# Sliding-window attention and a GEGLU block on one core: attention of the next batch interleaved by hand with an FFN group, sums by a ones matmul

## Chip, core and metric

One core of a Trainium2 chip runs the whole program. The metric is the device time of one execution in microseconds (us), as the median of several runs; every profile here is of one execution.

## What is computed

Eight batches of eight heads, 576 tokens of 64 features each, go through attention with a window of 128 tokens and a bias that grows with distance (ALiBi). The result, seen as 4608 tokens of 512 features, goes through a gated feed-forward block (FFN) of width 1536.

```python
scores = scale * np.matmul(q, k.transpose(0, 1, 3, 2))
mask = (rel >= 0) & (rel < window)                 # rel = query - key, window 128
scores = np.where(mask, scores + bias[None], -1e9)
attn = np.exp(scores - max); attn = attn / (np.sum(attn) + 1e-09)
x = np.matmul(attn, v)                             # as (4608, 512)
out = (gelu(x @ w_gate) * (x @ w_val)) @ w_out     # (4608, 512) float32
```

## The kernel before

**Attention** (attention_bp, L104 to L214) takes two batches at a time. POOL issues the loads of q, k and v (L113, L132), which change float32 to bf16 on the way. TensorE (PE) transposes q and k in blocks of 128 tokens (L98), and evac (L88 to L93) copies them out of PSUM on ACT (L90) and DVE (L92) in turn. For each head there are five key blocks: two score matmuls (L158, one for each batch), an exp on ACT over both (L164), a multiplication with the exponential of bias and mask on DVE (L168). Then come the value matmuls (L185). There the probabilities are the stationary operand and the values move, 65 columns: 64 values and a column of ones, so that the 65th output column is the sum over the keys, one number per query. DVE takes the reciprocal of these sums, four columns on 128 partitions and one on 64 (L192, L193), and multiplies the outputs by them (L195, L201). The result has tokens on partitions, so it is transposed once more (L98) into xT, which has features on partitions.

**The FFN** (ffn_group, L216 to L246) takes 512 tokens, nine groups in all. For each of 12 blocks of the hidden width four matmuls make the gate (L222), ACT takes gelu (L227), four make the value (L231), DVE multiplies the two (L235). Then four token blocks take 12 matmuls each with w_out (L240), evac copies them out, SP stores them (L246). PSUM has eight banks: three for scores, two for attention outputs, two for gate and value, one for the FFN's output (L45 to L48).

**Order.** The calls at the end (L248 to L258) go: attention of batches 0 and 1, the weight loads (L249 to L251), FFN groups 0 and 1, attention of 2 and 3, groups 2 and 3, and so on, with groups 6, 7 and 8 at the end. The scheduler of the framework may move instructions within an engine's queue: it pulls transposes of the next pair of batches into the FFN.

Of the kernel before, what the change touches and what calls it, by code (L numbers as in the profile page):

```python
# [10 lines left out]
ALU = mybir.AluOpType  # L12


@with_exitstack
def kernel(
# [10 lines left out]
    nc = tc.nc  # L27
# [5 lines left out]
    NKT = (S + 127) // 128  # L33
    LAST = S - 128 * (NKT - 1)

    consts = ctx.enter_context(tc.tile_pool(name="consts", bufs=1))
    slab_pool = ctx.enter_context(tc.tile_pool(name="slabs", bufs=2))
    qkT_pool = ctx.enter_context(tc.tile_pool(name="qkT", bufs=3))
    v_pool = ctx.enter_context(tc.tile_pool(name="vp", bufs=3))
    pT_pool = ctx.enter_context(tc.tile_pool(name="pT", bufs=3))  # L40
    xnat_pool = ctx.enter_context(tc.tile_pool(name="xnat", bufs=2))
    r_pool = ctx.enter_context(tc.tile_pool(name="rp", bufs=4))
    ffn_sb = ctx.enter_context(tc.tile_pool(name="ffn_sb", bufs=3))
    out_sb_pool = ctx.enter_context(tc.tile_pool(name="out_sb", bufs=3))
    ps_sc = ctx.enter_context(tc.tile_pool(name="ps_sc", bufs=3, space=bass.MemoryType.PSUM))  # L45
    ps_o = ctx.enter_context(tc.tile_pool(name="ps_o", bufs=2, space=bass.MemoryType.PSUM))
    ps_gv = ctx.enter_context(tc.tile_pool(name="ps_gv", bufs=2, space=bass.MemoryType.PSUM))
    ps_out = ctx.enter_context(tc.tile_pool(name="ps_out", bufs=1, space=bass.MemoryType.PSUM))  # L48

    ident = consts.tile([128, 128], BF16)  # L50
    nc.gpsimd.memset(ident, 0.0)
    nc.gpsimd.affine_select(
        out=ident, in_=ident, compare_op=ALU.not_equal, fill=1.0,
        base=0, pattern=[[-1, 128]], channel_multiplier=1,
    )

# [6 lines left out]
    nc.gpsimd.affine_select(
        out=tmpl, in_=tmpl, compare_op=ALU.is_ge, fill=1e9,
        base=0, pattern=[[1, 256]], channel_multiplier=-1,
    )
    nc.gpsimd.affine_select(
        out=tmpl, in_=tmpl, compare_op=ALU.is_ge, fill=1e9,
        base=W - 1, pattern=[[-1, 256]], channel_multiplier=1,
    )  # L70
# [3 lines left out]
    init_pool.release()  # L74

    wg = consts.tile([128, 4, DFF], BF16)
    wv = consts.tile([128, 4, DFF], BF16)
    wo = consts.tile([128, 12, DM], BF16)

    xT = consts.tile([128, 4, NTOK], BF16)  # L80

    qspan = [(128 * j, min(256, S - 128 * j)) for j in range(NKT)]
    pslot = [256 * j for j in range(NKT)]
    PTW = 256 * (NKT - 1) + LAST

    evac_flip = [0]

    def evac(dst, src):  # L88
        if evac_flip[0] % 2 == 0:
            nc.scalar.copy(out=dst, in_=src)  # L90
        else:
            nc.vector.tensor_copy(out=dst, in_=src)  # L92
        evac_flip[0] += 1  # L93

    def pe_transpose_block(ps_bf16, src):
        for j in range(NKT):
            sz = 128 if j < NKT - 1 else LAST
            nc.tensor.transpose(  # L98
                out=ps_bf16[:, 128 * j:128 * j + sz],
                in_=src(j, sz),  # L100
                identity=ident[0:sz, 0:sz],
            )

    def attention_bp(bp):  # L104
        bb = (2 * bp, 2 * bp + 1)
        qT, kT, vnat, xnat = {}, {}, {}, {}
        for b in bb:
            qsb = slab_pool.tile([128, NKT, DM], BF16, name="qsb")
            ksb = slab_pool.tile([128, NKT, DM], BF16, name="ksb")
            for sb, src in ((qsb, q), (ksb, k)):  # L110
                for j in range(NKT):
                    sz = 128 if j < NKT - 1 else LAST
                    nc.gpsimd.dma_start(  # L113
                        out=sb[0:sz, j, :].rearrange("p (h d) -> p h d", h=H),
                        in_=src[b][:, 128 * j:128 * j + sz, :].rearrange(
                            "h p d -> p h d"),
                    )

            qT[b] = qkT_pool.tile([128, 4, S], BF16, name="qT")
            kT[b] = qkT_pool.tile([128, 4, S], BF16, name="kT")  # L120
            for sb, dst in ((qsb, qT[b]), (ksb, kT[b])):
                for c in range(4):
                    pst = ps_sc.tile([128, 512], FP32, name="sc")
                    pstb = pst.bitcast(BF16)
                    pe_transpose_block(
                        pstb, lambda j, sz: sb[0:sz, j, 128 * c:128 * (c + 1)])
                    evac(dst[:, c, :], pstb[:, 0:S])

            vsb = slab_pool.tile([128, NKT, DM], BF16, name="vsb")
            for j in range(NKT):  # L130
                sz = 128 if j < NKT - 1 else LAST
                nc.gpsimd.dma_start(  # L132
                    out=vsb[0:sz, j, :].rearrange("p (h d) -> p h d", h=H),
                    in_=v[b][:, 128 * j:128 * j + sz, :].rearrange(
                        "h p d -> p h d"),
                )
            vnat[b] = v_pool.tile([128, NKT, H, 65], BF16, name="vp")
            nc.vector.memset(vnat[b][:, :, :, 64:65], 1.0)  # L138
            nc.vector.tensor_copy(
                out=vnat[b][:, 0:NKT - 1, :, 0:64],  # L140
                in_=vsb[:, 0:NKT - 1, :].rearrange("p j (h d) -> p j h d", h=H),
            )
            nc.vector.tensor_copy(
                out=vnat[b][0:LAST, NKT - 1, :, 0:64],
                in_=vsb[0:LAST, NKT - 1, :].rearrange("p (h d) -> p h d", h=H),
            )
            xnat[b] = xnat_pool.tile([128, NKT, DM], BF16, name="xnat")

        for h in range(H):
            hc, hp = h // 2, (h % 2) * 64  # L150
            pT = pT_pool.tile([128, 2, PTW], BF16)
            for j in range(NKT):
                kp = 128 if j < NKT - 1 else LAST
                q0, nq = qspan[j]
                sc = ps_sc.tile([128, 512], FP32, name="sc").rearrange(
                    "p (x n) -> p x n", x=2)
                for i, b in enumerate(bb):
                    nc.tensor.matmul(  # L158
                        out=sc[0:kp, i, 0:nq],
                        lhsT=kT[b][hp:hp + 64, hc, 128 * j:128 * j + kp],  # L160
                        rhs=qT[b][hp:hp + 64, hc, q0:q0 + nq],
                        start=True, stop=True,
                    )
                nc.scalar.activation(  # L164
                    out=pT[0:kp, :, pslot[j]:pslot[j] + nq],
                    in_=sc[0:kp, :, 0:nq], func=AF.Exp, scale=0.125,
                )
                nc.vector.tensor_tensor(  # L168
                    out=pT[0:kp, :, pslot[j]:pslot[j] + nq],
                    in0=pT[0:kp, :, pslot[j]:pslot[j] + nq],  # L170
                    in1=emask[0:kp, h:h + 1, 0:nq].to_broadcast((kp, 2, nq)),
                    op=ALU.mult,
                )

            for i, b in enumerate(bb):
                opp = ps_o.tile([128, NKT, 65], FP32, name="opp")
                for qt in range(NKT):
                    qs = 128 if qt < NKT - 1 else LAST
                    mms = []
                    if qt > 0:  # L180
                        mms.append((qt - 1, pslot[qt - 1] + 128))
                    mms.append((qt, pslot[qt]))
                    for mi, (j, col) in enumerate(mms):
                        kp = 128 if j < NKT - 1 else LAST
                        nc.tensor.matmul(  # L185
                            out=opp[0:qs, qt, :],
                            lhsT=pT[0:kp, i, col:col + qs],
                            rhs=vnat[b][0:kp, j, h, :],
                            start=(mi == 0), stop=(mi == len(mms) - 1),
                        )  # L190
# [98 lines left out]
```

## Time and profile before

| What | Value |
|---|---|
| Time, median of 3 runs | 528.34 us (527.97 to 529.66) |
| Span of the profiled execution, first to last instruction | 527.3 us |
| PE busy, share of the span | 487.2 us, 92% |
| DVE busy | 205.2 us, 39% |
| ACT busy | 188.4 us, 36% |
| POOL busy | 105.7 us, 20% |

The page gives no other time of the profiled execution than its span. Busy times of PE contain the time that a matmul takes to run through, and matmuls overlap, so 92% does not mean that PE streams at its peak. A group of instructions is named by engine and line of the kernel above; "idle before" is the time its engine stood still ahead of it, with what ended that.

### The profile page before, as it was taken

To read this page: it belongs to the slowest core of one execution; us is meant where nothing else is said; L and a number is where in the kernel's file an instruction comes from. 1 tells how busy PE (TensorE), PEld (TensorE's weight loads), DVE (VectorE), ACT (ScalarE), POOL (GpSimd) and SP (SyncE) were. 2 spreads that over 40 slices of the span, in tenths; PEclk is the share of its full clock that TensorE was granted. 3 is DMA by queue.
4 is the path that set the end of the run, shared out by engine and by line. 5 is a ranking of instruction groups with operands and counts; after the bars stand their busy time and mean duration, and the time that the engine had idled before them with its cause. 6 is when DMAs were issued, how large, how long until landed. Compare 5 with 4: busy or idle time off the path is not lost.

```text
span 527.3 us, 6826 instructions
## 1 busy us (share of the span) xinstructions
PE 487.2 (92%) x2638; PEld 239.9 (45%) x2672; DVE 205.2 (39%) x614; ACT 188.4 (36%) x350; POOL 105.7 (20%) x133
## 2 busy tenths in 40 slices
PE   3499899999989899999899999999899899999995
PEld 1255554444555544444555544444455434444432
DVE  0255644333354653142345643232354633232331
ACT  3166243132365243122565152132565232132220
POOL 9961796300440030002720000000000000000000
PEclk9999999999955589999955599999855589999999
DMA  9999999910990070102990000101100000201102
GB/s 88 138 178 210 158 142 101 106 40 2 125 90 1 0 47 0 61 20 31 167 63 2 0 1 1 73 8 41 42 0 1 0 1 0 81 1 41 40 0 81
DMA packets 120336, 28.76 MB, mean 55 GB/s; under 512 B 113136, under 2 KB 114672, under 8 KB 120304
## 3 DMA queue, kind: packets, MB, share of 16 engines
q0 software_dynamic: 115120, 18.88, 47.2%
q1 hardware_dynamic: 5184, 9.44, 4.7%
q8 instruction: 21, 0.34, 0.3%
q14 instruction: 11, 0.09, 0.0%
HBM read 37.75 MB, written 9.44 MB: 89 GB/s over the span
## 4 chain that ended last, share of the span: by engine, by line
PE 80%; DMA 6%; POOL 5%; ACT 4%; DVE 3%; issue 1%; another core or an unknown queue 1%; DVEq 0%; POOLq 0%; ACTq 0%
PE gv L231 20%; PE gv L222 17%; PE po L240 17%; PE opp L185 10%; PE sc L158 8%; PE sc L98 7%; DMA wv<-in_moe_w_val_dram 4%; DMA ksb<-in_k_dram 2%; POOL ksb L113 2%; POOL vsb L132 2%; POOL qsb L113 1%; ACT pT L164 1%; DVE hT L235 1%; ACT L164 1%
## 5 line engine op out<-in xcount | busy, mean ns | idle before, releaser
L235 DVE TENSOR_TENSOR hT<-gv,gelu 128x512 bf16<-128x512 f32 x108 | 74.7, 692 | 116.3 <-PE gv L231 111.9
L222 PE MATMUL gv<-xT,wg 128*128 128x512 bf16 x419 | 112.9, 388 | 2.4 <-ACT gelu L227 2.0
L231 PE MATMUL gv<-xT,wv 128*128 128x512 bf16 x420 | 112.6, 385 | 2.3 <-DVE hT L235 1.0
L227 ACT ACTIVATE gelu<-gv 128x512 bf16<-128x512 f32 x108 | 64.5, 597 | 133.5 <-PE gv L222 124.4
L240 PE MATMUL po<-wo,hT 128*128 128x512 bf16 x423 | 98.5, 379 | 2.7 <-ACT osb L90 1.3
L164 ACT ACTIVATE pT<-sc 128x512 bf16<-128x512 f32 (+2 forms) x160 | 71.2, 513 | 44.0 <-PE sc L158 27.5
L158 PE MATMUL sc<-qT,kT 64*128 64x256 bf16 (+2 forms) x320 | 75.0, 354 | 6.1 <-ACT pT L164 5.2
L185 PE MATMUL opp<-vp,pT 128*128 128x65 bf16 (+2 forms) x576 | 75.6, 246 | 4.3 <-DVE xnat L201 4.1
L231 PEld LDWEIGHTS <-wv 128*128 128x128 bf16 x432 | 42.4, 98 | 65.7 <-issue 27.5
L185 PEld LDWEIGHTS <-pT 128*128 128x128 bf16 (+2 forms) x576 | 46.9, 122 | 42.3 <-issue 11.8
L222 PEld LDWEIGHTS <-wg 128*128 128x128 bf16 x432 | 42.0, 98 | 52.3 <-issue 3.6
L240 PEld LDWEIGHTS <-hT 128*128 128x128 bf16 x432 | 41.8, 98 | 52.0 <-issue 4.0
L168 DVE TENSOR_TENSOR pT<-pT,emask 128x512 bf16<-128x512 bf16 (+2 forms) x160 | 48.5, 359 | 6.1 <-ACT pT L164 5.6
L113 POOL DMA_DIRECT2D qsb<-in_q_dram x40 | 34.4, 897 | 59.3 <-PE sc L98 59.1
L113 POOL DMA_DIRECT2D ksb<-in_k_dram x40 | 33.8, 888 | 54.4 <-PE sc L98 35.7
L92 DVE COPY osb<-po 128x512 f32<-128x512 f32 x18 | 12.5, 692 | 80.4 <-PE po L240 75.1
L132 POOL DMA_DIRECT2D vsb<-in_v_dram x40 | 34.0, 895 | 47.2 <-DVE vp L138 38.6
L158 PEld LDWEIGHTS <-kT 64*128 64x128 bf16 (+1 forms) x320 | 31.2, 122 | 26.0 <-issue 10.2
L192 DVE RECIPROCAL r<-opp 128x4 f32<-128x4 f32 x64 | 10.8, 176 | 61.5 <-PE opp L185 61.0
L90 ACT COPY osb<-po 128x512 f32<-128x512 f32 x18 | 10.5, 585 | 67.5 <-PE po L240 64.5
L98 PE MATMUL sc<-ident,qsb 128*128 128x128 bf16 (+1 forms) x160 | 19.2, 242 | 14.5 <-DMA qsb<-in_q_dram 13.2
L90 ACT COPY xT<-sc 128x576 bf16<-128x576 bf16 x16 | 10.2, 638 | 46.3 <-PE sc L98 46.3
(33 smaller groups left out, 198.4 us busy)
## 6 DMA issues: line engine op xcount, KB each, us to landing
out_dram<-osb SPq DMA_DIRECT2D x36, 256.0 KB, 2.0
qsb<-in_q_dram POOLq DMA_DIRECT2D x32, 128.0 KB, 4.4
ksb<-in_k_dram POOLq DMA_DIRECT2D x32, 128.0 KB, 4.9
vsb<-in_v_dram POOLq DMA_DIRECT2D x32, 128.0 KB, 4.1
wg<-in_moe_w_gate_dram POOLq DMA_DIRECT2D x1, 1536.0 KB, 12.1
wv<-in_moe_w_val_dram POOLq DMA_DIRECT2D x1, 1536.0 KB, 18.7
wo<-in_moe_w_out_dram POOLq DMA_DIRECT2D x1, 1536.0 KB, 25.6
qsb<-in_q_dram POOLq DMA_DIRECT2D x8, 64.0 KB, 4.0
```

The lines of the kernel that those rows point to most:

```text
L98: nc.tensor.transpose(out=ps_bf16[:, 128 * j:128 * j + sz], in_=src(j, sz), identity=ident[0:sz, 0:sz],)
L113: nc.gpsimd.dma_start(out=sb[0:sz, j, :].rearrange("p (h d) -> p h d", h=H), in_=src[b][:, 128 * j:128 * j + sz, :].rearrange("h p d -> p ...
L132: nc.gpsimd.dma_start(out=vsb[0:sz, j, :].rearrange("p (h d) -> p h d", h=H), in_=v[b][:, 128 * j:128 * j + sz, :].rearrange("h p d -> p h ...
L158: nc.tensor.matmul(out=sc[0:kp, i, 0:nq], lhsT=kT[b][hp:hp + 64, hc, 128 * j:128 * j + kp], rhs=qT[b][hp:hp + 64, hc, q0:q0 + nq], start=T ...
L164: nc.scalar.activation(out=pT[0:kp, :, pslot[j]:pslot[j] + nq], in_=sc[0:kp, :, 0:nq], func=AF.Exp, scale=0.125,)
L168: nc.vector.tensor_tensor(out=pT[0:kp, :, pslot[j]:pslot[j] + nq], in0=pT[0:kp, :, pslot[j]:pslot[j] + nq], in1=emask[0:kp, h:h + 1, 0:nq] ...
L185: nc.tensor.matmul(out=opp[0:qs, qt, :], lhsT=pT[0:kp, i, col:col + qs], rhs=vnat[b][0:kp, j, h, :], start=(mi == 0), stop=(mi == len(mms) ...
L222: nc.tensor.matmul(out=pg, lhsT=wg[:, c, 128 * f:128 * (f + 1)], rhs=xT[:, c, t0:t0 + 512], start=(c == 0), stop=(c == 3),)
L227: nc.scalar.activation(out=gelu, in_=pg, func=AF.Gelu)
L231: nc.tensor.matmul(out=pv, lhsT=wv[:, c, 128 * f:128 * (f + 1)], rhs=xT[:, c, t0:t0 + 512], start=(c == 0), stop=(c == 3),)
L235: nc.vector.tensor_tensor(out=hT[:, f, :], in0=pv, in1=gelu, op=ALU.mult)
L240: nc.tensor.matmul(out=po, lhsT=hT[:, f, 128 * t:128 * (t + 1)], rhs=wo[:, f, :], start=(f == 0), stop=(f == 11),)
```

## The change

The kernel is rewritten, with the order of the five engines' instructions fixed by hand (the order in the program is the order in each queue). Attention handles one batch and, within it, a pair of heads (c = 0 to 3) at a time. q and k are transposed as before. Keys are shifted by 64, so that the five key blocks meet 192, 256, 256, 256 and 128 queries (NQ). Score matmuls of the two heads alternate between the upper and lower 64 rows of the array and write two banks. Value matmuls have the values as the stationary operand, 64 columns for each head in its own half of the array's columns, and the probabilities move; the output comes out with features on partitions, as xT wants it, so the transposes after attention go. The sums over keys come from a second set of the same matmuls with a matrix of ones as stationary operand: every one of 64 partitions of a head then holds the sum of each query. Thus the reciprocal runs over 320 and 256 columns on 128 partitions. Eight PSUM banks are one pool. The mask of key blocks 0, 3 and 4 has its own table, emask2. Attention of batch g+1 runs within FFN group g: its transposes between the blocks of gate and value, the rest between halves of the output matmuls (6 each). Groups 7 and 8 have no attention beside them. The column ones and the weights' loads in four slices are set up at the start.

```diff
+NQ = (192, 256, 256, 256, 128)
+Q0 = (0, 64, 192, 320, 448)
+PCOL = (768, 0, 256, 512, 960)
+QS = 320
...
+    ctx.enter_context(tc.manual_schedule(
+        engines={ENG.PE, ENG.Activation, ENG.DVE, ENG.Pool, ENG.SP}))
...
+    psum = ctx.enter_context(
+        tc.tile_pool(name="psum", bufs=8, space=bass.MemoryType.PSUM))
+    def bank():
+        return psum.tile([128, 512], FP32, name="ps")
...
+    def score(b, c, i, j, ps, col):
+        lo = 64 * i
+        nc.tensor.matmul(
+            out=ps[:, col:col + NQ[j]],
+            lhsT=kT[b % 2][lo:lo + 64, c, 128 * j:128 * j + 128],
+            rhs=qT[b % 2][lo:lo + 64, c, Q0[j]:Q0[j] + NQ[j]],
+            start=True, stop=True)
...
+    def scores0(b, c):
+        ps = [bank(), bank()]
+        for m in (0, 1):
+            for i in (0, 1):
+                score(b, c + m, i, 4, ps[i], 128 * m)
+        for i in (0, 1):
+            exp(P[:, :, i, 960:1088], ps[i][:, 0:256].rearrange("p (m n) -> p m n", m=2))
+    def scores1(b, c):
+        ps = [bank(), bank()]
+        for j in (1, 2):
+            for i in (0, 1):
+                score(b, c, i, j, ps[i], PCOL[j])
+        for i in (0, 1):
+            exp(P[:, i, 0:512], ps[i])
+        mask(P[:, :, 0:512].rearrange("p i (n x) -> p i n x", n=2),
+             emask[:, 2 * c:2 * c + 2, :].unsqueeze(2).to_broadcast((128, 2, 2, 256)))
+    def scores2(b, c):
+        ps = [bank(), bank()]
+        for j in (0, 3):
+            for i in (0, 1):
+                score(b, c, i, j, ps[i], PCOL[j] - 512)
+        for i in (0, 1):
+            exp(P[:, i, 512:960], ps[i][:, 0:448])
+        mask(P[:, :, 512:1088], emask2[:, 2 * c:2 * c + 2, :])
+    def values(b, c):
+        x, y, z = bank(), bank(), bank()
+        for what in (0, 1):
+            for j in range(5):
+                for (a, e, ps, base) in (
+                        (Q0[j], min(Q0[j] + NQ[j], QS), (x, z)[what], 0),
+                        (max(Q0[j], QS), Q0[j] + NQ[j], y, 256 * what - QS)):
...
+                    for i in (0, 1):
+                        col = PCOL[j] + a - Q0[j]
+                        w = (vb[b % 2][:, j, 64 * (2 * c + i):64 * (2 * c + i) + 64]
+                             if what == 0 else ones)
+                        nc.tensor.matmul(
+                            out=ps[64 * i:64 * i + 64, base + a:base + e],
+                            lhsT=w, rhs=P[:, i, col:col + e - a],
+                            start=first, stop=last, skip_group_check=True)
+        r = r_pool.tile([128, S], FP32, name="r")
+        nc.vector.reciprocal(r[:, 0:QS], z[:, 0:QS])
+        nc.vector.tensor_tensor(out=xT[:, c, t0:t0 + QS], in0=x[:, 0:QS],
+                                in1=r[:, 0:QS], op=ALU.mult)
+        nc.vector.reciprocal(r[:, QS:S], y[:, 256:512])
+        nc.vector.tensor_tensor(out=xT[:, c, t0 + QS:t0 + S], in0=y[:, 0:256],
+                                in1=r[:, QS:S], op=ALU.mult)
...
+    load_qk(0)
...
+    load_v(0)
...
+    for h in range(H):
+        nc.scalar.activation(out=emask[:, h, :], in_=tmpl, func=AF.Exp, scale=-slope)
+    nc.vector.tensor_copy(out=emask2[:, :, 0:256], in_=emask)
+    nc.vector.memset(emask2[0:64, :, 256:448], 0.0)
+    nc.vector.tensor_copy(out=emask2[64:128, :, 256:448], in_=emask[64:128, :, 64:256])
+    nc.vector.tensor_copy(out=emask2[:, :, 448:576], in_=emask[:, :, 0:128])
+    for s in range(4):
+        load_w(step * s, step * (s + 1))
+    load_qk(1)
+    load_v(1)
+    nc.gpsimd.dma_start(out=wo, in_=moe_w_out.rearrange("(c p) f -> p c f", p=128))
+    for c in range(4):
+        if c % 2 == 0:
+            for m in (c, c + 1):
+                transposes(0, m)
+                transposes(0, 4 + m)
+            scores0(0, c)
+        scores1(0, c)
+        scores2(0, c)
+        if c:
+            values(0, c - 1)
+    values(0, 3)
+    for g in range(NG):
+        b = g + 1
+        if 1 < b < B:
+            load_qk(b)
+            load_v(b)
+        for f in range(NF):
+            gate_val(g, f)
+            if b < B and 2 <= f < 10:
+                transposes(b, f - 2)
+        if b < B:
+            scores0(b, 0)
+            scores1(b, 0)
+            out_half(g, 0)
+            scores2(b, 0)
+            out_half(g, 1)
+            scores1(b, 1)
+            out_half(g, 2)
+            scores2(b, 1)
+            values(b, 0)
+            out_half(g, 3)
+            scores0(b, 2)
+            scores1(b, 2)
+            out_half(g, 4)
+            scores2(b, 2)
+            values(b, 1)
+            scores1(b, 3)
+            out_half(g, 5)
+            scores2(b, 3)
+            values(b, 2)
+            out_half(g, 6)
+            values(b, 3)
+            out_half(g, 7)
+        else:
+            for u in range(8):
+                out_half(g, u)
```

transposes, gate_val and out_half do the same work as the old transposes, gate and value blocks and output blocks; out_half(g, u) is 6 of the 12 matmuls of token block u // 2, and the second half of each is copied out by DVE or ACT in turn and stored.

## Rows read from the trace of the kernel before

**Rows 1.** The page: span, busy time of PE and DVE, granted clock in 40 slices

```profile
span 527.3 us, 6826 instructions
...
PE 487.2 (92%) x2638; PEld 239.9 (45%) x2672; DVE 205.2 (39%) x614; ACT 188.4 (36%) x350; POOL 105.7 (20%) x133
...
PEclk9999999999955589999955599999855589999999
```

**Rows 2.** Stretches: start:end, length, busy of PE, PEld, DVE, ACT, POOL, clock, DMA

```profile
66.67:144.34 77.67, 76.60 (x385) 35.83 (x392) 27.97 (x54) 23.75 (x39) 31.46 (x38) 1.00 0.99 85
144.34:183.79 39.45, 36.22 (x243) 20.86 (x244) 21.77 (x99) 20.73 (x44) 6.69 (x9) 0.53 0.48 32
...
523.33:527.30 3.97, 0.00 (x0) 0.00 (x0) 0.69 (x1) 0.00 (x0) 0.00 (x0) 1.00 0.17 66
```

**Rows 3.** The chain that ended last: start, length, what; FFN matmuls

```profile
78.01 1.01 PE gv L231 x4
79.02 0.86 PE gv L222 x4
79.89 1.01 PE gv L231 x4
...
99.20 2.59 PE po L240 x12
```

**Rows 4.** Reciprocals that follow each other, near 60.24 us: groups of instructions

```profile
L192 DVE RECIPROCAL r<-opp 128x4 f32<-128x4 f32 x1 | 0.2, 154 | 0.0
L193 DVE RECIPROCAL r<-opp 64x1 f32<-64x1 f32 x1 | 0.1, 128 | 0.0
```

**Rows 5.** One line's instructions: all reciprocals of L192 and of L193, minimum/median/maximum

```profile
L192 DVE RECIPROCAL r<-opp x64: 154/182/184, 34.3 to 415.8; 128x4 f32<-128x4 f32 x64
...
L193 DVE RECIPROCAL r<-opp x64: 127/140/152, 34.4 to 416.3; 64x1 f32<-64x1 f32 x64
```

**Rows 6.** Groups by line and shape, whole run, DVE and ACT

```profile
L195 DVE TENSOR_TENSOR xnat<-opp,r 128x256 bf16<-128x256 f32 x64 | 25.6, 399 | 0.0
L201 DVE TENSOR_TENSOR xnat<-opp,r 64x64 bf16<-64x64 f32 x64 | 13.2, 206 | 0.0
L168 DVE TENSOR_TENSOR pT<-pT,emask 128x512 bf16<-128x512 bf16 x96 | 37.2, 412 | 6.1 <-ACT pT L164 5.6
L168 DVE TENSOR_TENSOR pT<-pT,emask 64x128 bf16<-64x128 bf16 x32 | 6.8, 212 | 0.0
L92 DVE COPY osb<-po 128x512 f32<-128x512 f32 x18 | 12.5, 692 | 80.4 <-PE po L240 75.1 <-remote 5.3
L164 ACT ACTIVATE pT<-sc 128x512 bf16<-128x512 f32 x96 | 52.5, 597 | 41.6 <-PE sc L158 25.8 <-PE opp L185 14.3 <-DVE xnat L201 0.3
L92 DVE COPY qT<-sc 128x576 bf16<-128x576 bf16 x16 | 7.3, 453 | 27.9 <-PE sc L98 27.9
L139 DVE COPY vp<-vsb 128x2048 bf16<-128x2048 bf16 x8 | 6.4, 801 | 1.6 <-DMA vsb<-in_v_dram 1.6
```

**Rows 7.** Stretches of 2 us: start:end, length, PE busy (x), clock, DMA share, GB/s

```profile
144.00:146.00 2.00, 1.38 (x12) 1.00 1.21 145
146.00:148.00 2.00, 1.32 (x12) 0.58 2.27 144
...
186.00:188.00 2.00, 2.00 (x18) 0.68 0.00 0
```

**Rows 8.** PE in order of time, merged: start, length, what

```profile
138.31 1.20 PE L98 MATMUL sc<-ident,qsb 128*128 128x128 bf16 x12
...
151.85 1.60 PE L158 MATMUL sc<-qT,kT 64*128 64x256 bf16 x7
```

**Rows 9.** POOL and ACT in order of time, at the start

```profile
6.89 4.22 POOL L113 DMA_DIRECT2D ksb<-in_k_dram  x5
...
4.57 2.56 ACT L73 ACTIVATE emask<-tmpl 128x256 bf16<-128x256 f32 x8 [2.55 <-POOL tmpl L67]
```

**Rows 10.** DMA issues: what, engine, count, KB each, us to landing

```profile
wv<-in_moe_w_val_dram POOLq DMA_DIRECT2D x1, 1536.0 KB, 18.7
```

More of the change, by code (lines that the diff above doesn't have):

```diff
@@ new lines, in load_v, with load_w @@
+    def load_v(b):
+        t = vb[b % 2]
+        for j in range(5):
+            lo = 64 if j == 0 else 0
+            nc.gpsimd.dma_start(
+                out=t[lo:128, j, :].rearrange("p (h d) -> p h d", h=H),
+                in_=v[b][:, 128 * j - 64 + lo:128 * j + 64, :].rearrange("h p d -> p h d"),
+            )
+    def load_w(lo, hi):
+        for dst, src in ((wg, moe_w_gate), (wv, moe_w_val)):
+            nc.gpsimd.dma_start(
+                out=dst[:, :, lo:hi],
+                in_=src[:, lo:hi].rearrange("(c p) f -> p c f", p=128))
@@ new lines, with evac, transposes @@
+    flip = [0]
+    def evac(dst, src):
+        if flip[0] % 2 == 0:
+            nc.vector.tensor_copy(out=dst, in_=src)
+        else:
+            nc.scalar.copy(out=dst, in_=src)
+        flip[0] += 1
+    def transposes(b, i):
+        nm, c = (("qsb", "ksb")[i // 4], i % 4)
+        src = slabs[nm, b]
+        ps = bank().bitcast(BF16)
+        for j in range(5):
+            sz = min(128, S - 128 * j)
+            nc.tensor.transpose(
+                out=ps[:, 128 * j:128 * j + sz],
+                in_=src[0:sz, j, 128 * c:128 * (c + 1)],
+                identity=ident[0:sz, 0:sz])
+        dst = qT[b % 2][:, c, :] if nm == "qsb" else kT[b % 2][:, c, 64:64 + S]
+        evac(dst, ps[:, 0:S])
@@ new lines, with exp, mask @@
+    probs = {}
+    def score(b, c, i, j, ps, col):
[5 more added lines that the diff above has]
+            start=True, stop=True)
+    def exp(dst, src):
+        nc.scalar.activation(out=dst, in_=src, func=AF.Exp, scale=0.125)
+    def mask(dst, m):
+        nc.vector.tensor_tensor(out=dst, in0=dst, in1=m, op=ALU.mult)
@@ new lines, with gate_val @@
+    hid = {}
+    def gate_val(g, f):
+        if f == 0:
+            hid[g] = h_pool.tile([128, NF, 512], BF16, name="hT")
+        t0 = 512 * g
+        pg, pv = bank(), bank()
+        for w, ps in ((wg, pg), (wv, pv)):
+            for c in range(4):
+                nc.tensor.matmul(
+                    out=ps, lhsT=w[:, c, 128 * f:128 * (f + 1)],
+                    rhs=xT[:, c, t0:t0 + 512], start=(c == 0), stop=(c == 3))
+        gl = g_pool.tile([128, 512], BF16, name="gelu")
+        nc.scalar.activation(out=gl, in_=pg, func=AF.Gelu)
+        nc.vector.tensor_tensor(out=hid[g][:, f, :], in0=pv, in1=gl, op=ALU.mult)
@@ new lines, with out_half @@
+    acc = {}
+    def out_half(g, u):
+        t, half = u // 2, u % 2
+        if half == 0:
+            acc[g] = bank()
+        po = acc[g]
+        for f in range(6 * half, 6 * half + 6):
+            nc.tensor.matmul(
+                out=po, lhsT=hid[g][:, f, 128 * t:128 * (t + 1)],
+                rhs=wo[:, f, :], start=(f == 0), stop=(f == NF - 1))
+        if half == 1:
+            osb = o_pool.tile([128, DM], FP32, name="osb")
+            evac(osb, po)
+            r0 = 512 * g + 128 * t
+            nc.sync.dma_start(out=out[r0:r0 + 128, :], in_=osb)
@@ L61 @@
+    tmpl = consts.tile([128, 256], FP32, name="tmpl")
     nc.gpsimd.iota(relt, pattern=[[1, 256]], base=0, channel_multiplier=-1)
     nc.gpsimd.tensor_copy(out=tmpl, in_=relt)
[L63 to L70, printed above, removed]
+    for base, step, chan in ((0, 1, -1), (W - 1, -1, 1)):
+        nc.gpsimd.affine_select(
+            out=tmpl, in_=tmpl, compare_op=ALU.is_ge, fill=1e9,
+            base=base, pattern=[[step, 256]], channel_multiplier=chan)
@@ L71 @@
+    load_v(0)
+    for i in range(2):
+        nc.vector.memset(kT[i][:, :, 0:64], 0.0)
+        nc.vector.memset(vb[i][0:64, 0, :], 0.0)
+    nc.vector.memset(ones, 1.0)
     for h in range(H):
```

236 lines of the change are left out of this document (46 added, 190 removed).

## Prediction

> **What bounds the kernel now.** The first view to read is the busy time of each engine: PE 92%, DVE 39% [rows 1]. The second is the run by stretches. The first FFN group starts at 66.67 us; a pair of groups takes 77.7 us, the attention between two pairs 39.4 us [rows 2]. The run is 66.7 + 77.7 + 39.4 + 76.8 + 39.0 + 77.0 + 39.1 + 107.7 + 4.0 us; stretches that repeat those shown are not listed. [...] The third view is the chain that ended last. Twelve output matmuls take 2.59 us, 216 ns each, with nothing between; one block of gate and value, eight matmuls, takes 1.88 us (79.89 - 78.01), where eight at 216 ns would take 1.73 [rows 3]. The difference is the two banks that gate and value share.
>
> **What goes.** Attention as a stage of its own goes (three times 39 us, and one of two batches at the start). The 160 transposes after it go. Eight banks take the wait out of gate and value, 12 x 0.145 = 1.7 us a group. All this is worth having only if what replaces attention fits beside the FFN.
>
> **What comes: the reciprocal.** Before, DVE inverted one number for each query and head, 5 columns per head. Now it inverts 320 + 256 columns for each head pair and batch: 32 x 576 = 18,432 columns in all. The trace has this operation at one and at four columns only. The two that follow another reciprocal directly took 128 and 154 ns [rows 4]: 26 ns for three columns, 8.7 ns each, and 119 ns fixed. Bounds: over all of them the medians, 140 and 182 ns, give 14 ns a column, but mix instructions that stand behind different ones [rows 5]; the lower end is the rate of the DVE multiplication from PSUM, (399 - 206) / 192 = 1.0 ns a column, 142 ns fixed [rows 6]. I take 8.7, as the only pair in one setting. So 320 columns take 2.90 us and 256 take 2.35; the multiplications behind them take 0.46 and 0.40 by their line, 0.07 less each where the next instruction starts under them. One step of values(b, c) holds DVE for 2.90 + 0.39 + 2.35 + 0.33 = 6.0 us, a batch for 23.9 us.
>
> [...]
>
> **The gate stage of a group.** 96 x 0.216 = 20.7 us. Beside it 40 transposes of the next batch: twelve took 1.20 us, less 0.25 for the last one's run-through 0.086 each [rows 8], so 3.4 us. DVE has 12 multiplications and 4 copies here and is covered. When FFN groups came back at 183.79 the clock was still low and reached a mean of 0.68 in 186 to 188 [rows 7]; three us at half speed cost 1.5 us. I charge that to each group, because PE waits before it (below): 25.6 us, between 24.1 and 25.6.
>
> **The out stage of a group.** PE: 48 x 0.216 = 10.4 us, plus scores of 2,176 columns and values of 4,352 columns in each of four steps. Nothing in the trace shows two heads side by side in the array. Bounds: at 0.42 ns a column [rows 3] and paired, 0.46 and 0.92 us a step; unpaired at the lower clock, where seven score matmuls of 256 took 1.6 us [rows 8], 1.8 and 3.7. I take 0.5 and 2.0, paired with something lost to loads and changes of form. PE's sum is then 20 us. DVE's queue is longer. A mask of 1,024 columns costs, by the line through 412 and 212 ns [rows 6], 0.68 us, and of 1,152 0.75 (0.62 and 0.69 with overlap). DVE has eight masks, two copies of 0.69 and four value steps: 5.3 + 1.3 + 23.9 = 30.5 us. So DVE sets this stage, and where it stands idle counts too:
>
> - Lead. The first reciprocal needs values(b, 0), and in DVE's queue it stands behind the second step's masks. PE does three output halves (3.9 us) and four score groups before; then two exps of 0.6 [rows 6] and a mask follow. Between 6.8 and 8.3 us; I take 8.0.
> - Work from there: 23.9 + four masks and a copy, 3.3.
> - Waits. If the eight banks go round in order, scores2(b, 2) takes the banks that the first reciprocals read, and scores2(b, 3) the bank of the copy behind the second; after each DVE waits for scores, exps and mask, 1.1 and 1.8 us less what it has to do. With values on PE at the lower clock 3.6 in all, with free banks 0. I take 1.8.
>
> Sum 37.0 us. The next gate stage needs all four c of xT and starts only when the last step is done. Group g reaches 512 - 64 g tokens into batch g, so groups 3 to 7 need only the first 320, and 2.35 + 0.33 = 2.7 us of the last step lie under the gate stage, five times: -13.5.
>
> **The start.** POOL issues ten loads first, 0.84 us each (4.22 for five), then makes the mask's template; ACT's eight exps take 2.56 us [rows 9], and DVE builds emask2 (four instructions; 2,048 columns took 0.80 [rows 6]). In DVE's queue all this stands ahead of the first copies of q: ready at 0.7 + 8.4 + 2 + 2.6 + 3.2 = 17 us. Two steps of copies, scores, exps and masks lead to the first reciprocal at 25.5; three steps with copies (0.45 each), masks and waits of 2 us between, and the fourth step, end at 57.5 us. Weights are hidden: a load took 18.7 us to land [rows 10], and they are issued from 15 to 22 us. Later loads of q, k, v are issued long before their use; POOL waits for nothing else. ACT's exps, gelus and table loads lie under DVE.
>
> **Sum.** Start 57.5; seven groups with attention 7 x (25.6 + 37.0) = 438.2; -13.5; groups 7 and 8, 144 x 0.216 = 31.1 each, and 1.5 for the clock: 63.7; the tail as before, 4.0 [rows 2]. 549.9 us against the span of 527.3. The median of the runs lies 1.0 above the span, so 551 us. Per two batches: 125 us where the kernel before takes 117.
>
> **Rivals.**
>
> Forecast, chance 0.62: DVE's reciprocals set the out stage; own range 528 to 580, from the bounds of lead, waits and clock (about 3 us a group) and a slope some 8% off.
>
> The reciprocal streams, chance 0.07: one column per 1.0 ns, the four columns of the trace being slow for another reason (they lie 65 apart). DVE then has 13 us in the out stage, PE's 22 us set it. Start 40, group 24.1 + 22.4: 40 + 326 + 62 + 4 = 432 us. 17,152 columns are on the path, so the change breaks even where a column costs 23 us / 17,152 = 1.3 ns less than I take, 7.3 ns. Against it stands the 26 ns for three columns. [...]
>
> Better cover, chance 0.14: as forecast, with lead 6.8, no bank waits and no low clock. 7 x (24.1 + 34.0) = 407; 57.5 + 407 - 13.5 + 62.2 + 4 = 517 us.
>
> Clock, chance 0.12: PE waits for DVE three times in a stage, 3 to 7 us. In the trace the clock fell to 0.58 within 2 us of a stretch with PE busy 1.38 of 2 us [rows 7]. If it falls at the first wait, two value steps take 1.9 us more ahead of DVE: 7 x 3.8 = 27 more, 577 us.
>
> The pairs do not run side by side, chance 0.05: 2 us more in the lead and for two value steps, 7 x 6: 593 us.
>
> **Chances and range.** A measurement of this kernel tells about 0.3% (1.6 us) from no change. Faster: the streaming reciprocal, 0.13 of better cover, 0.01 of the forecast's low end: 0.21. Same 0.04, where forecast and better cover meet. Slower 0.75. The range 512 to 592 leaves out 432 us, the slope of 14 ns, which would give over 630, and most of the last rival.
>
> **What the profile will show.** Right: reciprocals of 320 columns near 2.9 us; DVE full from the first reciprocal of an out stage to its last; the first gate matmul of the next group released by DVE; PE idle by several us there; about 62 us from group to group, 31 for the last two. Wrong: reciprocals under 1 us, or PE still the engine that others wait for in the out stage; slope right and time under 528 if the lead or waits are shorter; over 590 if values take 4 us a step.

## The result and the profile after

The changed kernel takes 484.75 us in the median of four runs (482.83 to 485.19), the kernel before on the same chip 528.15 (527.34 to 529.66): a ratio of 0.917, with an interval of 0.914 to 0.920. It is 43.4 us faster, where 551 us was forecast. The profiled execution took 485.19 us, 1.8 more than its span.

The page of the changed kernel: span, busy times, granted clock, and the chain that ended last by engine.

```profile
span 483.4 us, 6661 instructions
...
PE 406.9 (84%) x2704; PEld 197.4 (41%) x2704; DVE 293.8 (61%) x360; ACT 190.8 (39%) x342; POOL 110.4 (23%) x138
...
PEclk9995799969997899979997999799989999799999
...
PE 57%; DVE 36%; ACT 3%; POOL 2%; issue 2%; POOLq 0%
```

Against [rows 1], PE's busy time fell by 80 us and DVE's rose by 89. The long valleys of the clock have become short dips, and DVE carries 36% of the chain.

Next the stretches, with the columns of [rows 2]: the start; gate and out stage of the second group; gate and out stage of the fourth, like which the later ones are.

```profile
0.00:48.34 48.34, 19.57 (x180) 12.92 (x181) 29.59 (x38) 16.29 (x34) 37.71 (x52) 0.88 1.62 143
...
104.47:130.44 25.97, 25.97 (x137) 12.06 (x137) 9.07 (x15) 11.21 (x18) 7.46 (x9) 0.92 0.46 30
130.44:159.84 29.40, 21.92 (x187) 10.60 (x188) 25.92 (x27) 11.40 (x23) 5.13 (x7) 0.88 0.64 71
212.73:236.65 23.92, 23.92 (x135) 11.60 (x136) 11.10 (x17) 11.10 (x18) 7.45 (x9) 1.00 0.55 43
236.65:263.94 27.29, 21.80 (x188) 10.60 (x188) 23.88 (x26) 11.41 (x23) 5.14 (x7) 0.87 0.65 67
```

In the gate stage PE is busy from end to end; in the out stage it stands idle for 5 to 9 us while DVE is full from its first reciprocal on. Groups with attention take 56.1, 55.4 and 52.9 us, then four times 51.2; two batches cost 102.4 us late in the run, where the kernel before took 117.1 [rows 2].

The chain of the changed kernel through one out stage (start, length, what):

```profile
137.80 2.08 DVE r L195
...
139.90 0.49 DVE xT L196
140.39 1.68 DVE r L198
...
142.09 0.42 DVE xT L199
142.52 1.27 DVE P L137 x2
...
159.37 0.43 DVE xT L199
...
159.84 6.36 PE ps L211 x21
```

From 137.8 us to 159.8 the path runs through DVE alone, and the last multiplication of the fourth step releases the next group's matmuls (all but the first three, which need c = 0 to 2 alone and run at 154.91). That is the mechanism forecast. What differs is the length of a reciprocal. The groups of instructions of DVE, by shape:

```profile
L195 DVE RECIPROCAL r<-ps 128x320 f32<-128x320 f32 x32 | 68.8, 2150 | 0.0
L198 DVE RECIPROCAL r<-ps 128x256 f32<-128x256 f32 x32 | 55.9, 1748 | 0.0
L137 DVE TENSOR_TENSOR P<-P,emask 128x1152 bf16<-128x1152 bf16 x32 | 24.1, 755 | 8.1 <-ACT P L134 8.1
L137 DVE TENSOR_TENSOR P<-P,emask 128x1024 bf16<-128x1024 bf16 x32 | 22.0, 688 | 18.1 <-ACT P L134 17.9
L196 DVE TENSOR_TENSOR xT<-ps,r 128x320 bf16<-128x320 f32 x32 | 15.7, 492 | 1.1
L199 DVE TENSOR_TENSOR xT<-ps,r 128x256 bf16<-128x256 f32 x32 | 13.6, 425 | 1.1
```

Masks and multiplications came within 0.04 us of the forecast (0.75 and 0.68, 0.46 and 0.40 us). The reciprocals took 2.15 and 1.75 us instead of 2.90 and 2.35: (2150 - 1748) / 64 = 6.3 ns a column and some 140 ns fixed.

### The profile page after: what moved, and what is told of

It reads as the page before. It is cut to its first block, busy times and chain, and to the rows that moved or that the text cites. A ratio compares the mean times of both kernels' runs of the same rounds, so it can differ in the third digit from the quotient of the medians.

```text
span 483.4 us, 6661 instructions
## 1 busy us (share of the span) xinstructions
PE 406.9 (84%) x2704; PEld 197.4 (41%) x2704; DVE 293.8 (61%) x360; ACT 190.8 (39%) x342; POOL 110.4 (23%) x138
## 4 chain that ended last, share of the span: by engine, by line
PE 57%; DVE 36%; ACT 3%; POOL 2%; issue 2%; POOLq 0%
PE ps L211 40%; DVE r L195 14%; PE ps L226 10%; DVE r L198 9%; DVE P L137 5%; PE ps L116 4%; DVE xT L196 3%; ACT P L134 2%; PE ps L127 2%; DVE xT L199 2%; POOL qsb L81 1%; DVE osb L105 1%; POOL ksb L81 1%; ACT emask L256 1%; DVE qT L105 0%
## 5 line engine op out<-in xcount | busy, mean ns | idle before, releaser
L216 DVE TENSOR_TENSOR hT<-ps,gelu 128x512 bf16<-128x512 f32 x108 | 74.7, 692 | 128.9 <-PE ps L211 122.0
L211 PE MATMUL ps<-xT,wg 128*128 128x512 bf16 x432 | 120.3, 399 | 21.1 <-DVE xT L199 13.8
L211 PE MATMUL ps<-xT,wv 128*128 128x512 bf16 x432 | 114.6, 389 | 0.0
L226 PE MATMUL ps<-wo,hT 128*128 128x512 bf16 x432 | 111.5, 403 | 1.7 <-ACT osb L107 1.7
L215 ACT ACTIVATE gelu<-ps 128x512 bf16<-128x512 f32 x108 | 63.9, 597 | 112.6 <-PE ps L211 112.5
L134 ACT ACTIVATE P<-ps 128x512 bf16<-128x512 f32 (+2 forms) x160 | 73.7, 542 | 21.6 <-PE ps L127 21.6
L195 DVE RECIPROCAL r<-ps 128x320 f32<-128x320 f32 x32 | 68.8, 2150 | 0.0
L137 DVE TENSOR_TENSOR P<-P,emask 128x1024 bf16<-128x1024 bf16 x64 | 45.5, 721 | 26.2 <-ACT P L134 26.0
L90 POOL DMA_DIRECT2D vb<-in_v_dram x40 | 34.1, 870 | 100.3 <-PE ps L189 98.6
L198 DVE RECIPROCAL r<-ps 128x256 f32<-128x256 f32 x32 | 55.9, 1748 | 0.0
L127 PE MATMUL ps<-qT,kT 64*128 64x256 bf16 (+2 forms) x320 | 27.3, 272 | 5.6 <-DVE qT L105 5.4
## 6 DMA issues: line engine op xcount, KB each, us to landing
wo<-in_moe_w_out_dram POOLq DMA_DIRECT2D x1, 1536.0 KB, 12.6
```

Of the source, the lines that this page charges most:

```text
L127: nc.tensor.matmul(out=ps[:, col:col + NQ[j]], lhsT=kT[b % 2][lo:lo + 64, c, 128 * j:128 * j + 128], rhs=qT[b % 2][lo:lo + 64, c, Q0[j]:Q0 ...
L134: nc.scalar.activation(out=dst, in_=src, func=AF.Exp, scale=0.125)
L137: nc.vector.tensor_tensor(out=dst, in0=dst, in1=m, op=ALU.mult)
L195: nc.vector.reciprocal(r[:, 0:QS], z[:, 0:QS])
L198: nc.vector.reciprocal(r[:, QS:S], y[:, 256:512])
L211: nc.tensor.matmul(out=ps, lhsT=w[:, c, 128 * f:128 * (f + 1)], rhs=xT[:, c, t0:t0 + 512], start=(c == 0), stop=(c == 3))
```

## Experiments

Theory: the mechanism of the forecast holds, DVE's reciprocals set the out stage, and only their price was off; the gain over the kernel before comes mostly from PSUM banks that no longer hold PE up. Rivals: PE, exps or banks set the out stage, and the reciprocals are hidden; or interleaving alone is the gain.

### Each reciprocal twice

```diff
+        r2 = r_pool.tile([128, S], FP32, name="r2")
+        nc.vector.reciprocal(r2[:, 0:QS], z[:, 0:QS])
         nc.vector.reciprocal(r[:, 0:QS], z[:, 0:QS])
...
+        nc.vector.reciprocal(r2[:, QS:S], y[:, 256:512])
         nc.vector.reciprocal(r[:, QS:S], y[:, 256:512])
```

> Changed kernel with each reciprocal issued twice (the first result is not used). Theory (DVE's reciprocals set the out stage and the start, every column of them on the path): one more pair of 2.15 and 1.75 us per step, 3.76 us with the overlap of neighbours, 32 steps, less five hidden halves: +112 us, about 597 us; a little more if PE's longer waits bring the lower clock. Rival (the chain of scores, exp and mask or PE sets the stage and DVE has slack, 29.4 us less 25.9 busy in a stage): the first 3.5 us of each stage are free, +88 us or less, at most 573 us.

Measured 602.96 us (602.73 to 603.18), ratio to the kernel before 1.141 (1.136 to 1.146). The added instructions took 32 x (2.09 + 1.69) = 121 us, and the time rose by 118. The rival, which allows 88 at most, falls. By the chain of this run, all 32 first and 27 of the 32 second ones lie on the path, at 2.02 and 1.62 us each, 108 us in all; the five others are hidden, as forecast. The remaining 10 us are gate stages that got longer: those of the later groups take 25.2 to 26.7 us where the changed kernel has 23.9, and their first 21 matmuls by the chain 5.99 to 7.56 us instead of 4.69. They stand behind longer waits of PE (74.5 us ahead of its gate matmuls in the whole run, 21.1 in the changed kernel), and the run's mean clock is 0.858 where the changed kernel has 0.926.

### A copy in place of each reciprocal

```diff
-        nc.vector.reciprocal(r[:, 0:QS], z[:, 0:QS])
+        nc.vector.tensor_copy(out=r[:, 0:QS], in_=z[:, 0:QS])
...
-        nc.vector.reciprocal(r[:, QS:S], y[:, 256:512])
+        nc.vector.tensor_copy(out=r[:, QS:S], in_=y[:, 256:512])
```

> Changed kernel with a copy of the sums in place of each reciprocal, so the output is not normalised by the sums. Theory: a step of DVE falls from 4.72 to about 1.5 us, DVE's out stage to 13 us, and PE's sum of 18 us (10.4 output, 3.4 scores, 4.2 values) sets the stage; with a tail of about 2 us per stage it takes 20 instead of 29.4 or 27.3 us, the start loses 12 us: 405 to 420 us. Rival (latency of the chain sets the stage): 440 us or more.

This kernel leaves out the division by the sums. Measured 404.23 us (403.95 to 404.51), ratio 0.765 (0.761 to 0.768). The copies took 0.48 and 0.42 us, so DVE lost 32 x 3.0 = 96 us of work and the time 80.5 us. Two stretches of this kernel, a gate and an out stage (columns as above):

```profile
123.51:147.43 23.92, 23.92 (x135) 11.60 (x136) 9.07 (x15) 11.10 (x18) 8.84 (x11) 1.00 0.84 63
147.43:165.59 18.16, 18.16 (x186) 8.96 (x186) 13.32 (x26) 10.82 (x22) 2.87 (x5) 1.00 0.54 73
```

PE is now busy throughout, with its clock at 1.00: this is the floor that the reciprocals hide. Later groups follow each other every 42.6 us (by the chain, from 165.59 to 208.15) instead of 51.2: 8.6 us a group. Some 6 of the 80.5 us go with the clock: the first three gate stages take 23.9 us here, and 26.7, 26.0 and 25.6 in the changed kernel, at clocks of 0.89, 0.92 and 0.93.

### Reciprocals of several sizes by themselves

At the end of the changed kernel, after its last output, three reciprocals of each size from one bank (and from SBUF) were added:

```diff
+    mp = bank()
+    nc.vector.tensor_copy(out=mp, in_=mi)
+    for _ in range(3):
+        nc.vector.reciprocal(mo[:, 0:1], mp[:, 0:1])
...
+    for _ in range(3):
+        nc.vector.reciprocal(mo[:, 0:512], mp[:, 0:512])
...
```

> Changed kernel with reciprocals of chosen sizes added on DVE at its end, three of each in a row: 1, 4 adjacent, 4 columns 64 apart, 16, 64, 256 and 512 columns from PSUM, 512 and 1 from SBUF, 512 on 64 partitions. Theory A (one price per column at any width, what made it look dear before was the distance between the four columns): 6.3 ns a column everywhere, 4 adjacent columns 19 ns above 1 column, 4 apart 26. Theory B (the first columns cost more than later ones): 4 adjacent also 26 above 1, and the slope falls to 6.3 by 64 columns. SBUF as source: the same slope, if the divide and not the read sets it.

The instructions of the three smallest sizes (minimum/median/maximum in ns), then the groups of the others (mean ns of one behind the busy time; "ps" is PSUM, "mi" SBUF):

```profile
L326 DVE RECIPROCAL mo<-ps x3: 168/168/168, 478.3 to 478.7; 128x1 f32<-128x1 f32 x3
L328 DVE RECIPROCAL mo<-ps x3: 163/182/183, 478.8 to 479.2; 128x4 f32<-128x4 f32 x3
L330 DVE RECIPROCAL mo<-ps x3: 151/183/183, 479.3 to 479.7; 128x4 f32<-128x4 f32 x3
...
L332 DVE RECIPROCAL mo<-ps 128x16 f32<-128x16 f32 x3 | 0.7, 246 | 0.1
L334 DVE RECIPROCAL mo<-ps 128x64 f32<-128x64 f32 x3 | 1.6, 536 | 0.1
L336 DVE RECIPROCAL mo<-ps 128x256 f32<-128x256 f32 x3 | 5.2, 1736 | 0.1
L338 DVE RECIPROCAL mo<-ps 128x512 f32<-128x512 f32 x3 | 10.1, 3357 | 0.1
L340 DVE RECIPROCAL mo<-mi 128x512 f32<-128x512 f32 x3 | 10.1, 3353 | 0.1
L344 DVE RECIPROCAL mo<-ps 64x512 f32<-64x512 f32 x3 | 10.0, 3349 | 0.1
```

From 16 columns on the slope is 6.0 to 6.3 ns a column ((536 - 246) / 48, (1736 - 536) / 192, (3357 - 1736) / 256), and 512 columns take the same from PSUM (3357 ns) and SBUF (3353) and on half the partitions (3349). The first of each three stands behind another size and shows less than the other two (163 and 151 against 182 and 183), so that means of three mislead here. By the medians, three more columns make 14 ns adjacent (line 328) and 15 with the columns 64 apart (line 330): about 5 ns a column, in a row where each writes the same place as the one before. That is nearest to Theory A's 19 for adjacent columns, without its effect of distance; Theory B falls, and the 26 ns of [rows 4] for three columns did not come back.

### Small reciprocals, in rows of their own and in turn

The difference of 26 ns, on which the forecast rests, was still without a cause.

```diff
+    for n in range(6):
+        nc.vector.reciprocal(mo[:, 8 * n:8 * n + 4], mq[:, 0:4, 64])
...
+    for n in range(6):
+        nc.vector.reciprocal(mo[:, 256 + 8 * n:260 + 8 * n], mq[:, 0:4, 64])
+        nc.vector.reciprocal(mo[0:64, 260 + 8 * n:261 + 8 * n], mq[0:64, 4, 64:65])
```

> The changed kernel with small reciprocals from one bank at its end, each into a place of its own: six of four columns 65 apart on 128 partitions (line 325), six of one column on 64 partitions (line 327), six of one column on 128 (line 329), six of four adjacent columns (line 331), then six pairs in turn, four columns 65 apart and one column on 64 partitions (lines 333 and 334). The run before with three of each into one place gave 168 ns for one column and 172 to 176 for four, where the kernel before has 128 and 154 behind another reciprocal. Theory: what an instruction shows for so few columns is set by the instruction ahead of it, how far the two overlap, and not by the columns; then in rows of their own one and four columns differ by under 12 ns, and only the pairs in turn differ by 20 ns or more. Rival: the shape does it (64 partitions, or columns 65 apart); then line 327 is 20 ns or more under line 329, or line 325 as much over line 331, in rows of their own.

One execution, 482.5 us. The instructions by line, minimum/median/maximum in ns (each line number is one above what was written):

```profile
L334 DVE RECIPROCAL mo<-ps x6: 144/154/154, 477.6 to 478.3; 128x4 f32<-128x4 f32 x6
L335 DVE RECIPROCAL mo<-ps x6: 128/128/129, 477.7 to 478.4; 64x1 f32<-64x1 f32 x6
L326 DVE RECIPROCAL mo<-ps x6: 150/152/182, 476.0 to 476.4; 128x4 f32<-128x4 f32 x6
L332 DVE RECIPROCAL mo<-ps x6: 144/144/155, 477.2 to 477.6; 128x4 f32<-128x4 f32 x6
L330 DVE RECIPROCAL mo<-ps x6: 141/141/142, 476.8 to 477.1; 128x1 f32<-128x1 f32 x6
L328 DVE RECIPROCAL mo<-ps x6: 129/140/142, 476.4 to 476.8; 64x1 f32<-64x1 f32 x6
```

In turn (lines 334, 335) the pair of [rows 4] comes back, 154 and 128 ns in the median. In rows of their own, one column on 64 partitions takes 140 (line 328), four columns 65 apart 152 (326), four adjacent 144 (332). So of the 26 ns, 14 go when each follows its like, 8 when the columns lie side by side, and 3 to 4 are left for three columns. The rival falls, since partitions make 1 ns and distance 8, under its 20. The theory's 12 ns in rows of their own are just reached by the medians and passed by the means (156 and 139), in which the first instruction behind a copy counts with 182; so it is not confirmed as written, but what stands ahead is the larger part. These rows of six take about 0.5 us where six times 140 to 152 ns would be over 0.8, so neighbours overlap: what a short one shows is not its price.

### The kernel before with one pool of eight banks

```diff
-    ps_sc = ctx.enter_context(tc.tile_pool(name="ps_sc", bufs=3, space=bass.MemoryType.PSUM))
-    ps_o = ctx.enter_context(tc.tile_pool(name="ps_o", bufs=2, space=bass.MemoryType.PSUM))
-    ps_gv = ctx.enter_context(tc.tile_pool(name="ps_gv", bufs=2, space=bass.MemoryType.PSUM))
-    ps_out = ctx.enter_context(tc.tile_pool(name="ps_out", bufs=1, space=bass.MemoryType.PSUM))
+    psum = ctx.enter_context(tc.tile_pool(name="psum", bufs=8, space=bass.MemoryType.PSUM))
```

> Kernel before with one pool of eight PSUM banks for all its uses in place of 3 + 2 + 2 + 1; nothing else changes. Theory (most of the gain of the change is the FFN's freedom from bank waits: a pair of groups took 77.7 us where 2 x 31.1 of matmuls and 7 of transposes stand): 9 groups x about 4 us, 485 to 500 us. Rival (the gain is attention's time hidden beside the FFN): within 1% of 528 us.

Measured 493.99 us (493.33 to 494.37), ratio 0.934 (0.931 to 0.938). Nothing but the pools was edited, and 34.5 us of the change's 43.4 are there. But the framework's scheduler, which may move instructions in this kernel, places them otherwise with other pools: the stretch of two FFN groups contains 385 matmuls and transposes in [rows 2] and 291 here. So the run shows the banks together with the order that they allow. Stretches of this kernel: two FFN groups; the transposes and attention after them; the last three groups.

```profile
65.89:129.54 63.65, 63.65 (x291) 28.62 (x292) 22.60 (x35) 17.93 (x29) 23.00 (x28) 1.00 0.96 85
129.54:175.40 45.86, 42.48 (x346) 27.53 (x343) 27.97 (x117) 25.93 (x53) 16.74 (x20) 0.62 0.83 58
394.21:488.65 94.44, 94.42 (x433) 42.43 (x432) 28.81 (x42) 26.29 (x43) 0.00 (x0) 0.99 0.08 31
```

The last three groups took 107.7 us before and take 94.4. Not all of these 13.2 us are waits for banks, as PE's timeline of the kernel before shows (start, length, line, what):

```profile
417.28 3.13 PE L98 MATMUL sc<-ident,xnat 128*128 128x128 bf16 x25
...
477.54 2.75 PE L240 MATMUL po<-wo,hT 128*128 128x512 bf16 x12
...
510.19 2.75 PE L240 MATMUL po<-wo,hT 128*128 128x512 bf16 x12
513.61 2.53 PE L240 MATMUL po<-wo,hT 128*128 128x512 bf16 x11 [0.67 <-ACT osb L90]
```

The 25 transposes, 3.1 us, stand ahead of this stretch in the new order. From the outputs of one group to those of the next it is 32.65 us (477.54 to 510.19) before and 31.08 with one pool (416.11 to 447.19 by the chain): 1.6 us a group for gate and value, near the 1.7 of the prediction. In the last group each output block waits for the copy of the one ahead, 0.8 us (3.42 us from block to block against 2.59), three times.

Two batches take 63.65 + 45.86 = 109.5 us, 7.6 less than before. If PE's time is counted from each start to the next, gate, value and output take some 3 us less of it in these two batches, transposes and attention some 5, with the clock at 0.62 where [rows 2] has 0.53. Over the whole run, 19 of the 34.5 us lie in gate, value and output, 15 in transposes, scores and values. So the time that the theory gave was right, but its 4 us a group of FFN waits are about 2; what the pool brings to the old attention stood in no sum, and whether it comes from banks, order or clock is not taken apart.

### The changed kernel with its banks split again

```diff
-        tc.tile_pool(name="psum", bufs=8, space=bass.MemoryType.PSUM))
+        tc.tile_pool(name="psum", bufs=5, space=bass.MemoryType.PSUM))
+    ps_gv = ctx.enter_context(
+        tc.tile_pool(name="ps_gv", bufs=2, space=bass.MemoryType.PSUM))
+    ps_out = ctx.enter_context(
+        tc.tile_pool(name="ps_out", bufs=1, space=bass.MemoryType.PSUM))
```

> Changed kernel with its eight PSUM banks split again as before: two for gate and value, one for the output, five for attention. Theory (free banks are most of the gain): 0.145 us per block of gate and value, 12 x 9 of them, is 16 us, and the wait for the copy of an output block, about 0.85 us for 36 blocks, up to 30 us where attention's matmuls do not stand between: 505 to 525 us. Rival (the order by hand and the shared work make banks unimportant): under 495 us.

Measured 514.88 us (514.04 to 515.73), ratio 0.974 (0.970 to 0.979): 30 us above the changed kernel. The groups of instructions name the place, with the idle time of PE ahead of the output matmuls last:

```profile
L231 PE MATMUL po<-wo,hT 128*128 128x512 bf16 x432 | 113.9, 406 | 30.7 <-DVE osb L109 29.4 <-ACT osb L111 1.3
```

The one output bank waits for its copy out, which stands in DVE's queue among the reciprocals. The row names the place, not the sum: part of this wait takes the place of another, as PE's idle time ahead of the value matmuls falls from 32 to 9 us. Seen from both kernels, the shared banks are worth 30 to 35 us, though they lose them in different places.

### Attention behind the FFN group instead of inside it

```diff
         if b < B:
+            for u in range(8):
+                out_half(g, u)
             scores0(b, 0)
             scores1(b, 0)
-            out_half(g, 0)
             scores2(b, 0)
-            out_half(g, 1)
...
```

> Changed kernel with the eight output halves of a group put ahead of the attention of the next batch instead of between its parts; the same instructions otherwise. Theory (interleaving is worth what it hides of the output matmuls, since DVE's 22 us of a stage stay the same): a stage becomes 10.4 us of output matmuls, about 5.4 us to the first reciprocal (as at the start of the kernel, 18.3 to 23.7 us) and 22 us of DVE, less 2.1 where the last half is hidden: 37.9 and 35.8 us instead of 29.4 and 27.3, seven times 8.5 = +60 us, about 545 us, slower than the kernel before. Rival (order does not matter, DVE's sum sets the stage): within 2% of 485 us.

Measured 561.19 us (560.37 to 562.0), ratio 1.062 (1.058 to 1.067). The same instructions in another order cost 76 us more, so the interleaving is worth that much, and without it the new attention is slower than the old. Stretches of this kernel behind a gate stage: output, first scores and exps, values.

```profile
139.88:150.25 10.37, 10.37 (x52) 4.59 (x52) 2.07 (x3) 0.59 (x1) 0.93 (x2) 1.00 0.85 117
150.25:156.57 6.32, 2.67 (x38) 1.86 (x40) 2.14 (x4) 6.24 (x12) 0.00 (x0) 0.95 0.11 41
156.57:178.76 22.19, 9.38 (x105) 6.28 (x102) 21.86 (x21) 4.47 (x10) 4.19 (x5) 0.65 0.42 27
```

DVE's 22 us are the same; what comes ahead of them, 10.4 + 6.3, is now all exposed. The time lies 16 us above what was written, from two sources. The middle stretch was put at 5.4 us and takes 6.3, as ACT has a copy out and its table load of 1.28 us ahead of the exps: a stage takes 38.9 us instead of 37.9, some 7 us in seven. And the later groups start slowly, where those of the changed kernel don't: their first 21 matmuls take 5.96 to 7.48 us by the chain instead of 4.69 (as the 21 behind the third row, where the clock was 0.65, take 6.86), the last 93 take 22.93 instead of 20.23, 10 us in all, which are part of the 76.

### The second part of a step one stage later

If DVE is the bound in the out stage and has room in the gate stage (9 to 11 us busy of 24), the columns that the next group doesn't need can wait. QS becomes 512 - 64 b, at least 320; ACT copies the rest out of its bank; reciprocal and multiplication of the rest come behind the first four blocks of the next gate stage.

```diff
+        QS = max(320, 512 - 64 * b)
...
-        nc.vector.reciprocal(r[:, QS:S], y[:, 256:512])
...
+        nc.scalar.copy(out=ys[:, 0:2 * R], in_=y[:, 0:2 * R])
+        def rest():
+            nc.vector.reciprocal(r[:, QS:S], ys[:, R:2 * R])
...
+        todo.append(rest)
...
             gate_val(g, f)
+            if todo and f < 4:
+                todo.pop(0)()
```

> Changed kernel with the split of a batch at 512 - 64 b tokens (at least 320) in place of 320, and the reciprocal and product of the second part moved from the out stage into the next gate stage, behind the products of its blocks 0 to 3; ACT copies the bank of the second part out of PSUM so that it comes free. Theory (reciprocals are the end of the out stage, and the gate stage has DVE time free: 9 to 11 of 24 to 26 us busy): after a lead of 7.35 us DVE has 3.2 us of masks and copy and four first parts of 3.4, 3.0 or 2.6 us: stages of 24.2, 22.4 and five of 20.7 us in place of 29.4 twice and 27.3 five times, -45 us; start -3, clock -3: about 434 us. Rival (the work is only moved: DVE's later products hold up the gate stage, or ACT's four copies the exps): 465 us or more.

Measured 449.13 us in the median (443.87 to 450.70), ratio 0.851 (0.847 to 0.855): 36 us under the changed kernel and faster than both. It stays 15 us above the 434 written. Stretches of this kernel, three stages in a row and one gate stage behind them:

```profile
143.33:167.26 23.93, 23.93 (x136) 11.60 (x136) 15.07 (x23) 11.11 (x18) 7.46 (x9) 1.00 0.69 46
167.26:188.91 21.65, 18.87 (x188) 9.25 (x188) 17.74 (x19) 13.65 (x27) 5.13 (x7) 1.00 0.61 72
188.91:214.52 25.61, 25.61 (x135) 12.03 (x136) 16.91 (x23) 11.21 (x18) 7.45 (x9) 0.93 0.68 51
```

The out stage is down from 27.3 to 21.65 us, and PE still waits at its end for the last steps' reciprocals; some gate stages begin at a lower clock (0.93 in the third row). This profiled execution is the fastest, 443.87 us, 10 above the 434: the out stages are 6 us longer in all than written, and the 3 us of clock were not won. What makes the other executions 4 to 7 us longer stays open.

## Why the prediction was wrong

**Bound: right.** DVE's reciprocals set the out stage and the start; the twofold reciprocals and the copies show it from both sides. The lead, the steps and the order in the queue had the form described, down to DVE's release of the gate matmuls.

**The step that failed** is "I take 8.7, as the only pair in one setting". Measured are 6.3 ns a column. The forecast's own break-even was 7.3: the price alone turns the sign. A step's 576 columns cost 576 x 2.4 = 1.4 us less: 35.6 us on the path of the out stages (28 steps, less the five hidden second parts) and 5.5 at the start. The sum with 6.3 ns would be 549.9 - 41.1 = 508.8 us, 3.5% faster than before. The pair had too little of the operation in it: three columns among 119 ns fixed, and of its 26 ns more than half came from the two standing in turn, as the run with small reciprocals shows. The range of the slope, "some 8% off", was far too narrow for an extrapolation from 4 columns to 320; the bounds, 1.0 and 14, stood beside it, and held both signs. That the time fell so far below the range has a second reason: "better cover" stood as a rival of its own, with a chance of 0.14, but nothing kept a lower price and a better cover from coming together, and they did, the latter in part.

**Out stage, the other 14.6 us of seven stages.** These are the bank waits, 12.6, and the lead, 4.6, less 2.8 for the steps. The bank waits of 1.8 us didn't come: from its first reciprocal DVE has no gap. The third step's last scores, which that step of the working saw held up by the first step's reciprocals, ran at 140.52, under the second of them, with no wait in their row. The lead was 7.35 us (130.37 to 137.72), inside 6.8 to 8.3 and under the 8.0 taken. A step took 4.7 us, 0.1 over what 6.3 ns gives. The timeline of PE there (start, length, line, what):

```profile
135.93 0.66 PE L189 MATMUL ps<-P,vb 128*64 128x192 bf16 x12
136.42 0.64 PE L189 MATMUL ps<-P,ones 128*64 128x192 bf16 x12
...
140.52 0.36 PE L127 MATMUL ps<-qT,kT 64*128 64x192 bf16 x4
...
150.42 1.12 PE L189 MATMUL ps<-P,vb 128*64 128x192 bf16 x12 [3.76 <-DVE P L137]
```

The value matmuls of a step take 1.06 us (135.93 to 136.99), near the paired bound of 0.92, where 2.0 was taken; so the rival that the pairs do not run side by side is out.

**Clock.** It was charged to all seven gate stages at 1.5 us; three paid (26.7, 26.0 and 25.6 us at clocks of 0.89, 0.92 and 0.93), four didn't (23.9 at 1.00). Stretches of 2 us, with the columns of [rows 2]:

```profile
150.00:152.00 2.00, 1.58 (x22) 1.58 (x23) 2.00 (x2) 0.00 (x0) 0.91 (x2) 0.50 0.34 131
160.00:162.00 2.00, 2.00 (x6) 0.65 (x5) 0.00 (x0) 1.48 (x2) 0.00 (x0) 0.50 0.00 0
...
264.00:266.00 2.00, 2.00 (x10) 0.92 (x10) 1.97 (x2) 1.59 (x2) 0.00 (x0) 1.00 0.38 108
```

The clock does fall in the middle of an out stage, to 0.50 after PE stood idle from 146.6 to 150.4, and values then take 1.12 us for twelve instead of 0.66. That was the rival's mechanism, but its price didn't come: they are the fourth step's values, and DVE was at work on the third step's reciprocals beside them.

**The start** took 48.3 us instead of 57.5, 5.5 of the difference being the reciprocals; the first of them came at 23.7 us instead of 25.5. **The last two groups** took 61.7 (417.59 to 479.30) instead of 63.7, **the tail** 4.1 instead of 4.0 us. Over the run: 9.2 + 5.2 (gate stages) + 50.2 (out stages) + 1.9 = 66.5 us, the span's whole error.

**Where the gain comes from.** "All this is worth having only if what replaces attention fits beside the FFN" was right, but the smaller edit ahead of it was passed over: the banks. The prediction priced the FFN without waits, and so had their gain in its sum, yet spoke of 1.7 us a group. For gate and value that is about right (1.6). But one pool in the kernel before brings 34.5 of the 43.4 us, 15 of them in its old attention and transposes, which no term of the prediction weighs. The new attention, with its reciprocals, is worth the rest, 9 us beside free banks and 13 beside split ones (528.2 to 514.9).

## What to carry to other kernels

A price per element can't be taken from two instructions whose time is nearly all fixed: if no wide one is in the trace, forecast from both bounds and let the break-even speak. Before a stage is rebuilt to overlap better, ask which matmuls wait for a PSUM bank: one pool of eight banks, without any other edit, brought 6.6% here, in a kernel whose order the scheduler may change with it. And where one engine fills a stage and rests in the next, move what the next stage doesn't yet need: that brought 7% on top of the change.

## What the hardware showed

A reciprocal on DVE took 3357 ns for 512 columns from PSUM, 3353 from SBUF and 3349 on 64 partitions; from 256 columns to 512 that is 6.3 ns a column. Rows of short ones overlap, six of 140 to 152 ns in about 0.5 us: one column shows 128 ns behind four, 140 behind its like, and 168 where three in a row write the same place. Two heads in separate halves of the array's columns ran side by side: 24 value matmuls with 4,352 columns in 1.06 us are 0.24 ns a column, where an output matmul takes 0.42 [rows 3].
